# One weight's first step, two rests and one multiply moved on VectorE and GpSimd in the first MLP of a mixer and MLP kernel

## The chip, the cores and the metric

The kernel runs on one core of one Trainium2 chip. A core has a matrix engine (TensorE, called PE in the profile, with PEld for its weight loads), a vector engine (VectorE, DVE), an activation engine (ScalarE, ACT), GpSimd (POOL) and a queue engine that issues the transfers (SyncE, SP). Each works through its own instructions in order and waits for others by semaphores. The metric is the device time of one execution in microseconds (us), the median of several runs.

## The reference, cut to what matters

Three stages run behind each other on 4 batches: a gated linear attention with 8 heads of 48 columns over 768 steps, a mixer with a channel MLP of 1536 columns, and a gated spatial MLP.

```python
def _attn_ref(q, k, v, alpha):
    for t in range(S):
        state = alpha[:, :, t, :, None] * state + einsum('bhd,bhe->bhde', k[:, :, t], v[:, :, t])
        y[:, :, t] = einsum('bhd,bhde->bhe', q[:, :, t], state)

def _moe_ref(x, U, V, w_ch1, w_ch2):
    xt = x.transpose(0, 2, 1)
    h = xt @ U @ V
    u = x + h.transpose(0, 2, 1)
    ch = np.maximum(u @ w_ch1, 0.0) @ w_ch2
    return u + ch

def _moe2_ref(x, w_in, w_spatial, b_spatial, w_out):
    h = np.maximum(x @ w_in, 0.0)
    u, v = h[..., :512], h[..., 512:]
    v_n = (v - mean(v)) / np.sqrt(var(v) + 1e-06)
    v_s = einsum('ts,bsd->btd', w_spatial, v_n) + b_spatial[None, :, None]
    return (u * v_s) @ w_out
```

## The kernel before, in words

**Attention.** The 8 heads of a batch are 4 pairs of heads, so there are 16 pairs n, and batch 1 has the pairs 4 to 7 (in this text its first to fourth pair). `prepare(n)` makes running products of alpha: a scan backwards (`bw`, L914) with a reciprocal behind it (L917), and a scan forwards (`fw`, L927). `scale` (L903) multiplies k by `bw` and q by `fw`, on VectorE or on GpSimd: the variable `cut` says how much of it VectorE takes. In batch 1 VectorE takes k of the first three pairs and q of the third; GpSimd takes k of the fourth and q of the others. A pair then goes through PE in steps: k is turned (L958), what each chunk adds is made (L1002), VectorE scans it over the chunks (`state`, six scans, L1013), ScalarE lays the states out (L1023, L1024), PE makes scores (L974), VectorE masks them (L1091 for the third pair on, L984 before), and PE makes the outputs (L1103), which ScalarE takes (L1059). In the same steps the mixer of the pair before runs: two turns (L1213, taken by L1220), a product with U (L1229) into the bank that is called ALONE, and `keep`, which reads that bank on ScalarE (L1236) and VectorE (L1237). The turn of the next pair's k (L958) writes into ALONE as well, so it waits for L1237; L1229 waits for the six scans L1013, which read their decay out of ALONE.

**First MLP.** While batch 0's channel MLP runs on PE (up L380, ReLU L387 on ScalarE, the rest of h in `hl` L368 on VectorE, down L287 to L289, sum L440), the twelve weights come in as words of 64 bits and are made into two parts each, by hand-written steps. `begin` of a weight makes its 32-bit form on VectorE in three instructions (L237, L240, L247). `finish` is called twice for a weight: the first time ScalarE makes the high part (L785), the second time VectorE makes the rest (L252). L252 has both of its inputs in SBUF, and so has a multiply in L903.

**What sets the order.** The MLP calls `pull()` after every few matmuls, some 110 times and more in batch 0. At a pull (a hand-out) the table `FIRST_STEPS` says which weight steps are issued (`f` a finish, `b` a begin, `s` a step of the first batch's rest), and behind them, from pull 71 on, the steps of batch 1's attention are dealt out. Nothing reorders afterwards: each engine works in this order. The last `begin`, the twelfth weight's, is at pull 101, and the last three `finish` calls are at 107, 110 and 110. The eleventh weight's parts are called w_1459 and the twelfth's w_1619 in the lists below.

## Time and profile before

| what | before |
|---|---|
| median of 3 runs | 673.28 us (672.82 to 673.53) |
| the profiled execution | 674.17 us |
| its span, first to last instruction | 672.5 us |
| PE busy in the span | 658.3 us, 98% |
| VectorE, ScalarE, GpSimd busy | 425.3, 305.9 and 146.2 us |
| mean granted clock of TensorE | 0.997 of full speed |

The profile is of one execution, 0.89 us above the median of the runs. Times of rows count from the start of its span; 1.67 us of its time lie around the span. PE is busy nearly all the time, so what counts is where it is idle and who ends that. A row of the timeline has start, length, engine, line, operation, output and input tiles, shape and count; in brackets the idle time of the engine before it and what ended it. On VectorE an instruction's start is often recorded some 0.08 us before the one ahead of it ends.

### The profile page before, as it was taken

Reading aid. Unit: us, or ns where it says so; the run is one execution under the profiler, and the core shown is the slowest. Engines: PE = TensorE matmul, PEld = TensorE weight load, DVE = VectorE, ACT = ScalarE, POOL = GpSimd, SP = SyncE. Lnnn points to the kernel's source line nnn. Section 1 sums busy time; section 2 is a strip of 40 time slices with the busy share of each in tenths; the row PEclk is TensorE's granted clock in tenths of the full one; section 3 lists DMA queues with packets and bytes.
Section 4 is the critical chain, followed back from the end, with each engine's and each line's share of the span. In section 5 each row is a group of like instructions: output and inputs, shape, how many; then the busy total and the mean of one; then the engine's idle time right before and its main releaser. Section 6 shows DMA issues by size and latency. Waiting matters only on the chain.

```text
span 672.5 us, 13771 instructions
## 1 busy us (share of the span) xinstructions
PE 658.3 (98%) x5644; PEld 626.1 (93%) x5644; DVE 425.3 (63%) x813; ACT 305.9 (45%) x599; POOL 146.2 (22%) x138
## 2 busy tenths in 40 slices
PE   8999999899999999999999999999999999999995
PEld 7889999799999999999999999899999989999995
DVE  7989999867566336465327787495384356537441
ACT  3985467566455335555323444343344243334321
POOL 4530111232211231220110000306402520640141
PEclk9999999999999999999999999999999999999998
DMA  9699015562556502503023365401120202110011
GB/s 347 250 352 238 21 36 115 106 124 90 117 102 136 102 0 70 115 3 85 17 71 96 116 177 141 130 0 36 37 70 1 71 2 70 37 36 35 1 37 40
DMA packets 24039, 61.02 MB, mean 91 GB/s; under 512 B 3232, under 2 KB 13344, under 8 KB 22688
## 3 DMA queue, kind: packets, MB, share of 16 engines
q1 hardware_dynamic: 23968, 60.06, 32.6%
q8 instruction: 46, 0.75, 0.5%
q14 instruction: 25, 0.20, 0.1%
HBM read 47.47 MB, written 9.44 MB: 85 GB/s over the span
## 4 chain that ended last, share of the span: by engine, by line
PE 84%; DVE 8%; DMA 5%; issue 1%; ACT 1%; DVEq 0%; ACTq 0%; SPq 0%
PE banks L380 19%; PE banks L287 18%; PE banks L288 18%; PE banks L289 18%; DMA akq<-in_akq 5%; PE banks L1103 2%; DVE bw L914 1%; DVE fw L927 1%; PE banks L958 1%; PE banks L1002 1%; PE banks L974 1%; PE banks L1213 1%; PE banks L1175 1%; PE banks L1122 1%; DVE hl L368 1%
## 5 line engine op out<-in xcount | busy, mean ns | idle before, releaser
L380 PE MATMUL banks<-partuh,w 128*128 128x384 f32 x564 | 130.7, 339 | 1.4 <-DVE hl L368 1.3
L380 PEld LDWEIGHTS banks<-partuh,w 128*128 128x128 f32 x564 | 99.3, 188 | 3.5 <-DVE hl L368 2.2
L287 PE MATMUL banks<-h,w 128*128 128x384 f32 x288 | 98.1, 341 | 0.2
L289 PE MATMUL banks<-hl,w 128*128 128x384 f32 x288 | 96.4, 335 | 0.0
L288 PE MATMUL banks<-h,w 128*128 128x384 f32 x288 | 96.4, 335 | 0.0
L368 DVE SCALAR_TENSOR_TENSOR hl<-banks,h 128x384 fp32r<-128x384 f32 x96 | 52.7, 550 | 52.7 <-ACT h L387 52.1
L387 ACT ACTIVATE h<-banks 128x384 fp32r<-128x384 f32 x94 | 45.6, 486 | 76.4 <-PE banks L380 76.2
L252 POOL TENSOR_TENSOR partul<-ub,partuh 128x384 fp32r<-128x384 f32 x43 | 43.1, 1028 | 137.2 <-ACT partuh L457 84.7
L252 POOL TENSOR_TENSOR room<-room 128x384 fp32r<-128x384 f32 x32 | 32.5, 1017 | 163.2 <-ACT room L600 162.9
L380 PE MATMUL banks<-partul,w 128*128 128x384 f32 x282 | 66.1, 342 | 0.0
L287 PEld LDWEIGHTS banks<-h,w 128*128 128x128 f32 x288 | 54.1, 188 | 1.6 <-issue 0.8
L288 PEld LDWEIGHTS banks<-h,w 128*128 128x128 f32 x288 | 54.1, 188 | 0.0
L289 PEld LDWEIGHTS banks<-hl,w 128*128 128x128 f32 x288 | 54.1, 188 | 0.0
L903 POOL TENSOR_TENSOR akq<-akq,fw 128x768 f32<-128x768 f32 x13 | 22.5, 1730 | 135.1 <-DVE fw L927 86.6
L380 PEld LDWEIGHTS banks<-partul,w 128*128 128x128 f32 x282 | 49.2, 188 | 0.8
L600 ACT ACTIVATE room<-room 128x384 fp32r<-128x384 f32 x32 | 16.8, 526 | 66.8 <-DVE room L598 66.8
L252 DVE TENSOR_TENSOR vl<-vt,vh 128x512 fp32r<-128x512 f32 (+1 forms) x48 | 26.6, 617 | 20.7 <-ACT vh L505 20.7
L903 POOL TENSOR_TENSOR akq<-akq,bw 128x768 f32<-128x768 f32 x11 | 18.6, 1689 | 65.1 <-DVE bw L914 47.5
L289 PE MATMUL banks<-partul,winh 128*128 128x384 f32 x96 | 32.5, 338 | 0.0
L288 PE MATMUL banks<-partuh,winl 128*128 128x384 f32 x96 | 32.5, 338 | 0.0
L287 PE MATMUL banks<-partuh,winh 128*128 128x384 f32 x96 | 32.4, 338 | 0.0
L288 PE MATMUL banks<-wouth,room 128*128 128x384 f32 x96 | 32.3, 336 | 0.0
(256 smaller groups left out, 1498.3 us busy)
## 6 DMA issues: line engine op xcount, KB each, us to landing
akq<-in_akq SPq DMA_DIRECT2D x24, 434.4 KB, 7.6
bits<-in_w SPq DMA_DIRECT2D x12, 768.0 KB, 11.8
x2d<-ub SPq DMA_DIRECT2D x8, 576.0 KB, 3.4
ub<-x2d SPq DMA_DIRECT2D x8, 576.0 KB, 4.3
out_y<-room SPq DMA_DIRECT2D x24, 192.0 KB, 1.9
v<-in_v SPq DMA_DIRECT2D x15, 288.0 KB, 8.3
words<-in_wsT SPq DMA_DIRECT2D x7, 576.0 KB, 4.0
words<-in_w_in SPq DMA_DIRECT2D x8, 384.0 KB, 3.2
```

The lines of the kernel that those rows point to most:

```text
L252: engine.tensor_tensor(out=out, in0=x, in1=hi.bitcast(F32), op=ALU.subtract)
L287: nc.tensor.matmul(out=ps, lhsT=wh, rhs=xh, start=first, stop=False, skip_group_check=more)
L288: nc.tensor.matmul(out=ps, lhsT=wl, rhs=xh, start=False, stop=False, skip_group_check=more)
L289: nc.tensor.matmul(out=ps, lhsT=wh, rhs=xl, start=False, stop=last, skip_group_check=more)
L368: nc.vector.scalar_tensor_tensor(out=hl, in0=ps[:, 0:TB], scalar=0.0, in1=h.bitcast(F32), op0=ALU.max, op1=ALU.subtract)
L380: nc.tensor.matmul(out=ps[:, 0:TB], lhsT=wx[:, k * 128 : (k + 1) * 128], rhs=ux[:, k, :], start=i == 0, stop=i == len(parts) - 1)
L387: nc.scalar.activation(out=h, in_=ps[:, 0:TB], func=AF.Relu)
L600: nc.scalar.activation(out=hi, in_=x, func=AF.Copy)
L903: engine.tensor_tensor(out=chunks(x)[:, c], in0=chunks(x)[:, c], in1=chunks(by)[:, c, 1:CW], op=ALU.mult)
L914: nc.vector.tensor_tensor_scan(out=bw[:, ::-1], data0=a[:, 1 : AW + 1][:, ::-1], data1=ends[:, ::-1], initial=0.0, op0=ALU.mult, op1=ALU.max)
L927: nc.vector.tensor_tensor_scan(out=fw, data0=a[:, 0:AW], data1=starts, initial=0.0, op0=ALU.mult, op1=ALU.max)
L1103: nc.tensor.matmul(out=self.py[HW * h : HW * h + D, x, j * CH : (j + 1) * CH], lhsT=vw[:, h, c, :], rhs=self.sms[h][:, t], start=True, sto ...
```

## The change

The table hands out the last `begin` at pull 107 instead of 101, the rest of the eleventh weight at 110 instead of 107, and the rest of the twelfth at 113 instead of 110. The condition in `scale` gives VectorE the multiply of q by `fw` for the fourth pair too.

```diff
 FIRST_STEPS = {
     5: "f", 6: "b", 13: "fbf", 22: "fbf", 31: "fbf", 34: "ss", 40: "fbf", 49: "fbf", 51: "ss", 58: "f", 59: "f",
-    60: "b", 70: "ff", 80: "b", 89: "ff", 92: "b", 101: "fb", 107: "f", 110: "ff",
+    60: "b", 70: "ff", 80: "b", 89: "ff", 92: "b", 101: "f", 107: "b", 110: "ff", 113: "f",
 }
...
-            cut = NCH if n == 0 or by is bw and NP <= n < 2 * NP - 1 or by is fw and n == NP + 2 else 0
+            cut = NCH if n == 0 or by is bw and NP <= n < 2 * NP - 1 or by is fw and NP + 2 <= n < 2 * NP else 0
```

The first place is VectorE between the sums of the MLP (L440) and the correction L1237 of the first mixer product. Before:

```order
L440 TENSOR_TENSOR ub<-banks,ub 128x384 x3
L237 TENSOR_SCALAR narrow<-bits 128x768
L240 SCALAR_TENSOR_TENSOR narrow<-bits,narrow 128x768
L247 ISA narrow<-bits,narrow 128x1536
L1013 SCALAR_TENSOR_TENSOR after<-add,banks 128x96 x6
L1091 TENSOR_TENSOR akq_89<-banks,causal 64x6x64 x2
L1091 TENSOR_TENSOR sq<-banks,causal 64x6x64 x2
L368 SCALAR_TENSOR_TENSOR hl<-banks,h 128x384
L927 SCALAR_TENSOR_TENSOR fw<-akq_87,starts 128x780
L252 TENSOR_TENSOR w_1459<-narrow,w_1459 128x768
L1237 TENSOR_TENSOR stk<-banks,stk 32x128
```

The same place on VectorE in the changed kernel (akq_87 holds the fourth pair's k and q, akq_89 the third's):

```order
L440 TENSOR_TENSOR ub<-banks,ub 128x384 x3
L1013 SCALAR_TENSOR_TENSOR after<-add,banks 128x96 x6
L1091 TENSOR_TENSOR akq_89<-banks,causal 64x6x64 x2
L1091 TENSOR_TENSOR sq<-banks,causal 64x6x64 x2
L368 SCALAR_TENSOR_TENSOR hl<-banks,h 128x384
L927 SCALAR_TENSOR_TENSOR fw<-akq_87,starts 128x780
L903 TENSOR_TENSOR akq_87<-akq_87,fw 128x768
L237 TENSOR_SCALAR narrow<-bits 128x768
L240 SCALAR_TENSOR_TENSOR narrow<-bits,narrow 128x768
L247 ISA narrow<-bits,narrow 128x1536
L1237 TENSOR_TENSOR stk<-banks,stk 32x128
```

The three rows of the begin went from ahead of the six scans to behind the scan L927, the multiply L903 came in ahead of them, and L252 left the place ahead of L1237.

The second place is VectorE behind L1237, up to the fourth pair's scans and masks. Before:

```order
L1237 TENSOR_TENSOR stk<-banks,stk 32x128
L252 TENSOR_TENSOR w_1619<-narrow,w_1619 128x768
L368 SCALAR_TENSOR_TENSOR hl<-banks,h 128x384
L440 TENSOR_TENSOR ub<-banks,ub 128x384 x3
L914 SCALAR_TENSOR_TENSOR bw<-akq_88,ends 128x780
L917 RECIPROCAL starts<-bw 128x12
L1013 SCALAR_TENSOR_TENSOR after<-add,banks 128x96 x6
L1091 TENSOR_TENSOR akq_87<-banks,causal 64x6x64 x2
```

The same place in the changed kernel (akq_88 holds k and q of pair 8, the first of batch 2):

```order
L1237 TENSOR_TENSOR stk<-banks,stk 32x128
L252 TENSOR_TENSOR w_1459<-narrow,w_1459 128x768
L368 SCALAR_TENSOR_TENSOR hl<-banks,h 128x384
L440 TENSOR_TENSOR ub<-banks,ub 128x384 x3
L914 SCALAR_TENSOR_TENSOR bw<-akq_88,ends 128x780
L917 RECIPROCAL starts<-bw 128x12
L252 TENSOR_TENSOR w_1619<-narrow,w_1619 128x768
L1013 SCALAR_TENSOR_TENSOR after<-add,banks 128x96 x6
L1091 TENSOR_TENSOR akq_87<-banks,causal 64x6x64 x2
```

The rest of the eleventh weight now stands behind L1237, and that of the twelfth between pair 8's scan L914 and the fourth pair's scans L1013. On GpSimd the multiply of akq_87 by `fw` is gone and nothing else moves; the orders of PE, ScalarE and SyncE are what they were.

## Rows read from the trace of the kernel before

**Rows 1.** Stretch table: stretch, its length, busy of PE, PEld, DVE, ACT, POOL, clock, DMA.

```profile
143.00:665.00 522.00, 521.73 (x3934) 503.23 (x3933) 294.38 (x610) 212.42 (x422) 113.75 (x104) 1.00 0.25 67
```

**Rows 2.** Timeline of PE, 117 to 138 us, third and fourth pair.

```profile
117.60 0.93 PE L974 MATMUL banks<-akq 64*64 64x64 f32 x48
...
120.23 1.55 PE L1229 MATMUL banks<-yb,u 128*96 128x128 f32 x12 [0.98 <-DVE after L1013]
...
122.75 0.23 PE L1103 MATMUL banks<-akq,state 128*48 128x64 f32 x1 [0.37 <-DVE sq L1091]
...
127.51 0.84 PE L958 MATMUL banks<-ident,akq 128*128 128x128 f32 x6 [0.50 <-DVE stk L1237]
...
129.40 0.34 PE L289 MATMUL banks<-hl,w 128*128 128x384 f32 x1
...
137.34 0.23 PE L1103 MATMUL banks<-akq,state 128*48 128x64 f32 x1
```

**Rows 3.** Timeline of DVE, 116 to 134 us.

```profile
116.15 0.55 DVE L237 TENSOR_SCALAR narrow<-bits 128x768 uint32<-128x768 uint32 x1
...
118.61 1.57 DVE L1013 TENSOR_TENSOR_SCAN after<-add,banks 128x96 f32<-128x96 f32 x6
120.21 1.22 DVE L1091 TENSOR_TENSOR akq<-banks,causal 64x384 f32<-64x384 f32 x2
...
123.95 0.56 DVE L368 SCALAR_TENSOR_TENSOR hl<-banks,h 128x384 fp32r<-128x384 f32 x1 [1.35 <-ACT h L387]
124.42 1.77 DVE L927 TENSOR_TENSOR_SCAN fw<-akq,starts 128x780 f32<-128x780 f32 x1
126.11 0.93 DVE L252 TENSOR_TENSOR w<-narrow,w 128x768 fp32r<-128x768 f32 x1
127.08 0.28 DVE L1237 TENSOR_TENSOR stk<-banks,stk 32x128 fp32r<-32x128 f32 x1
127.77 1.64 DVE L252 TENSOR_TENSOR w<-narrow,w 128x768 fp32r<-128x768 f32 x1 [0.41 <-ACT w L785]
...
131.31 1.77 DVE L914 TENSOR_TENSOR_SCAN bw<-akq,ends 128x780 f32<-128x780 f32 x1
133.11 0.23 DVE L917 RECIPROCAL starts<-bw 128x12 f32<-128x12 f32 x1
133.26 1.51 DVE L1013 TENSOR_TENSOR_SCAN after<-add,banks 128x96 f32<-128x96 f32 x6
```

**Rows 4.** Timeline of ACT, 115 to 127 us.

```profile
115.44 0.70 ACT L1010 ACTIVATE add<-banks 128x576 f32<-128x576 f32 x1
120.21 1.14 ACT L1023 ACTIVATE state<-after 64x528 f32<-64x528 f32 x1 [4.07 <-DVE after L1013]
...
123.45 0.47 ACT L387 ACTIVATE h<-banks 128x384 fp32r<-128x384 f32 x1
...
126.22 0.27 ACT L1236 ACTIVATE stk<-banks 96x128 fp32r<-96x128 f32 x1
```

**Rows 5.** Timeline of DVE, the third pair's `fw` and q.

```profile
109.25 1.77 DVE L927 TENSOR_TENSOR_SCAN fw<-akq,starts 128x780 f32<-128x780 f32 x1
111.05 0.96 DVE L903 TENSOR_TENSOR akq<-akq,fw 128x768 f32<-128x768 f32 x1
111.93 0.55 DVE L368 SCALAR_TENSOR_TENSOR hl<-banks,h 128x384 fp32r<-128x384 f32 x1
```

**Rows 6.** Timeline of POOL: the fourth pair's q, and pair 8's k.

```profile
126.36 2.23 POOL L903 TENSOR_TENSOR akq<-akq,fw 128x768 f32<-128x768 f32 x1 [10.37 <-DVE fw L927]
133.21 1.68 POOL L903 TENSOR_TENSOR akq<-akq,bw 128x768 f32<-128x768 f32 x1 [4.62 <-DVE bw L914]
```

**Rows 7.** Timeline of POOL in the last stage.

```profile
467.52 1.98 POOL L654 TENSOR_TENSOR late<-late,bb 128x384 f32<-128x384 f32 x2
```

**Rows 8.** Timeline of DVE at the same time.

```profile
468.56 1.35 DVE L593 TENSOR_TENSOR room<-late 128x384 f32<-128x384 f32 x1 [1.73 <-POOL late L654]
```

**Rows 9.** What line L593 runs: count, ns least/median/most, first and last start, form.

```profile
L593 DVE TENSOR_TENSOR room<-late x8: 548/951/1357, 468.6 to 652.0; 128x384 f32<-128x384 f32 x8
```

## The prediction

> **What bounds the kernel now.** I read the stretch table first, then the timelines of PE, VectorE, ScalarE and GpSimd around 116 to 138 us, where the change lies. From 143 us to 665 us PE is busy for 521.73 of 522.00 us [rows 1]: whatever PE loses or wins before 143 us moves the end by the same amount, and nothing later takes it back. So the question is what the change does to PE's waits in the third and fourth pair of batch 1. There are three [rows 2]: 0.98 us ahead of the mixer product L1229 (for the six scans L1013), 0.37 us in the outputs L1103 (for the masks L1091), and 0.50 us ahead of the turn L958 (for L1237). The reader should see that all three releasers are VectorE rows, and that VectorE runs from 116.15 us to 127.36 us with one hole of 1.35 us, in which it waits for h [rows 3]. Here VectorE's queue sets the pace, not PE.
>
> **The begin, taken away ahead of the scans.** Its three instructions lie between 116.15 and 118.61 us, 2.46 us [rows 3]. Without them the scans can start when `add` is there: ScalarE's L1010 ends at 115.44 + 0.70 = 116.14 us [rows 4], so they start at about 116.17 us, 2.44 us earlier, and end at 117.74 us. L1229 then waits for nothing: PE is ready at 120.23 - 0.98 = 119.25 us. The masks need the scores, which end at 117.60 + 0.93 = 118.53 us [rows 2] and don't move; two pairs of masks take 123.95 - 1.35 - 120.21 = 2.39 us [rows 3], so they end at 120.96 us instead of 122.60, and the 0.37 us goes too. PE is then at the turn L958 some 0.98 + 0.37 = 1.35 us earlier, at 127.51 - 0.50 - 1.35 = 125.66 us or before. If that were all, the gain would be up to 0.98 + 0.37 + 0.50 = 1.85 us.
>
> **What it meets at L1237.** The turn L958 waits for L1237, and the begin now stands ahead of L1237, with one more multiply. Follow VectorE's queue. ScalarE starts its chain on the end of the scans (L1023 at 120.21 us, h at 123.45 us [rows 4]); all of it comes 2.44 us earlier, so `hl` L368 starts at 123.95 - 2.44 = 121.51 us, later than the masks' end and so still set by h. The scan L927 starts at 124.42 - 2.44 = 121.98 us. Multiplying q on VectorE is priced from the third pair [rows 5]: the multiply starts 111.05 - 109.25 = 1.80 us behind its scan and the next instruction 0.88 us behind that, so 123.78 and 124.66 us. The begin takes 2.46 us from there: L1237 starts at 127.12 us. Before it started at 127.08 us [rows 3]. In one sum: 2.44 us earlier into the chain, the rest L252 out of the way (127.08 - 126.11 = 0.97 us), and 0.94 us of multiply (the 0.88 us, and the 0.06 us more that an instruction waits which needs the scan's result) and 2.46 us of begin come in: +0.05 us or so. L1236 on ScalarE ended at 126.49 us [rows 4], some 0.6 us before L1237, and comes earlier now, so it doesn't decide. PE's turn starts at 127.55 us against 127.51 us, and the two waits that vanished come back as one of about 1.9 us in front of L958. Queued behind it on PE are the rest of the weight steps' matmuls and the fourth pair. **This part is worth nothing, 0.0 within 0.1 us.** The 0.1 is what single starts on VectorE differ by in rows of the same kind.
>
> **q of the fourth pair off GpSimd.** GpSimd's multiply took 2.23 us, 126.36 to 128.59 us [rows 6], and goes. Its readers are the scores, which PE runs behind the turn L958, and the copy of q into `sq` on SyncE's queue, which L1103 reads later still; the copy, and the loads queued behind it there, may start some 4 us earlier (124.7 instead of 128.6 us), but with the turn where it was an earlier q helps no one. But it had cost VectorE something: the rest L252 at 127.77 us took 1.64 us against 0.93 us for the same form at 126.11 us [rows 3], and it ended at 129.41 us, 0.82 us behind the multiply's end. So one of them stood still while the other ran. That 0.71 us goes, but PE doesn't wait there.
>
> The Trainium skill says of elementwise work (GPSIMD Engine Reference, Engine selection) that VectorE should have it, GpSimd being about 2 times slower on two inputs. The rows agree, 0.96 against 1.68 to 2.23 us; by that rule the move would gain 0.7 us or more, by the row of PE's wait it gains nothing, since VectorE is the engine that is short here.
>
> **The two rests.** w_1459's L252 now follows L1237, from about 127.3 to 128.3 us. Its reader, the eleventh weight's third group of matmuls, is ordered behind the second mixer turn and L1002, so it has time. `hl` and the three sums L440 follow; the last sum needs L289, which PE ends at 129.40 + 0.34 = 129.74 us [rows 2], 129.78 us now. From there pair 8's scan L914 can start at some 130.28 us (one sum's spacing is 0.46 us), a good 1 us before its 131.31 us [rows 3], and ends at 130.28 + 1.77 = 132.05 us.
>
> Now comes the place that decides. On the end of L914 GpSimd starts to multiply pair 8's k: 133.21 us, 0.13 us behind 131.31 + 1.77 = 133.08 us [rows 6], so at 132.18 us. VectorE's second instruction behind L914 starts 0.18 us behind it (L1013 at 133.26 us, 0.15 us behind L917's start [rows 3]), so at 132.23 us. Before, that was L1013, which reads one input from PSUM and ran along undisturbed. Now it is w_1619's L252, the very instruction that stood still beside GpSimd in the row above. Two bounds:
>
> - GpSimd comes first: L252 ends 0.82 us behind GpSimd's end, at 132.18 + 1.68 + 0.82 = 134.68 us, and the fourth pair's scans start 0.08 us before that, at 134.60 us instead of 133.26: 1.34 us later. Behind them on VectorE stand the four masks, and who waits for those is L1103. Before, scans and masks end at 133.26 + 1.51 + 0.03 + 2.39 = 137.19 us, and the L1103 that needs the last mask starts at 137.34 us [rows 2], 0.15 us behind it, just as at 122.60 and 122.75 us in the third pair: there is no room, and PE goes on 1.34 us later.
> - VectorE comes first: the scans start at 132.23 + 0.86 = 133.09 us, 0.17 us earlier, GpSimd waits, and nobody needs pair 8's k until the next batch. PE is then as before, 0.0 to -0.1 us.
>
> I take the first. GpSimd's start is 0.05 us ahead by the rows, and where the two came close in the last stage, GpSimd's second multiply (from about 468.49 to 469.50 us [rows 7]) was some 0.07 us ahead of VectorE's L593 at 468.56 us, and it was VectorE that stood: 1.35 us [rows 8] where the same form takes 0.55 us [rows 9]. But 0.05 us is the smallest lead of all, and both starts are worked out.
>
> The Trainium skill has the rule behind these rows (SBUF — State Buffer, Who interferes with whom): a VectorE instruction with two SBUF inputs and a GpSimd one that reads SBUF need the same port, and "Issue order, not op shape, decides who blocks." The trace agrees that one blocks whole (1.64 against 0.93 us); by the rule the sum is +1.34 us where GpSimd issues first. Another page (Perfetto Trace Analysis, DVE / Act Engine Instruction) says that VectorE's recorded start lies behind the start of its reading; no run here shows it, and by it the lead may be none and the sum 0.0 us.
>
> **The sum.** 0.0 us at L958 and +1.34 us at the fourth pair's scans. The profiled execution took 674.17 us, so 675.5 us; against the median, 673.28 + 1.34 = 674.6 us. That is slower by 0.199%, just at the 0.2% that a measurement of this kernel can tell from no change.
>
> **The rivals.**
>
> - *VectorE takes the port first.* Place: w_1619's L252 beside pair 8's k at 132.2 us. Price: 1.34 us less than the forecast, so 673.2 us, not slower. It decides within some 0.05 us: if L252 reads before GpSimd does. For it: the lead is tiny, and worked out from starts that may not mean the same on two engines. Against: rows 7 to 9.
> - *The chain to L1237 is shorter than worked out*, and part of the three waits is won: up to 1.85 us, 671.4 us; with L252 stalled as well, 672.8 us. For it: three edits at once, and PE is ready 1.9 us ahead. Against: every term of the queue has its row, and to win 1 us it would have to run a microsecond faster than it did.
> - *More is lost than the stall*: the start of the fourth pair's h and the first products of the mixer come late beyond the 1.34 us because ScalarE, too, gets out of step. Some 0.5 us more, 675.1 us. Nothing in the rows asks for it.
>
> That the instructions don't move as said is excluded by the lists of their order.
>
> **How the numbers follow.** Forecast 0.52, VectorE first 0.36, a shorter chain 0.06, more lost 0.06. The range goes from 672.8 us (VectorE first, less the 0.1 us of the chain and some 0.3 us of what runs differ by) to 675.2 us (the forecast and half a microsecond); it leaves out most of the third case and part of the last. Slower by over 0.2%: half of the forecast, 0.26, and most of the last, 0.05, so 0.31 in all. Within 0.2%: the other half, VectorE first, some of the third: 0.64. Faster: 0.05. The forecast's own range is 674.2 to 675.1 us.
>
> **What the profile after would show.** Right: PE's waits ahead of L1229 and L1103 of the third pair gone, one of some 1.9 us ahead of L958 at 127.5 us; L1237 at about 127.1 us behind L247; an L252 of about 2.4 us behind L917, and the fourth pair's scans at 134.6 us, with a new wait of PE in L1229 or L1103. Wrong: L252 there at 0.9 us and GpSimd's multiply at 2.4 us or so (then VectorE was first), or L1237 well before 127 us (then the queue was mis-sized, and the time falls).

## The result, and the profile after

The changed kernel takes 676.52 us (median of 8 runs, 675.77 to 680.10) where the kernel before, run beside it, takes 673.46 us (8 runs, 672.82 to 674.01): a ratio of 1.0058, 95% interval 1.0047 to 1.0070. It is slower by 3.1 us; the forecast was 674.6 us, in a range up to 675.2. Beside the later experiments it was 676.80 against 674.00 us, 1.0047 (1.0035 to 1.0059). The kernel before has few runs above 675 us in any comparison; the changed kernel has none below 675.5 in 15, and they spread far wider.

| what | before | after |
|---|---|---|
| the profiled execution | 674.17 us | 675.77 us |
| its span | 672.5 us | 674.1 us |
| PE busy in the span | 658.3 us | 658.5 us |
| mean granted clock of TensorE | 0.997 | 0.995 |

In the trace after, everything from 10 us to 110 us is some 0.3 us later than in the trace before, since the first input load came later; times below are as recorded, so 0.3 us of each difference is that.

PE first, from the third pair's end on (start, length, engine, line, operation, tiles, count, idle time ahead and who ended it):

```profile
119.44 1.47 PE L1229 MATMUL banks<-yb,u 128*96 128x128 f32 x12
...
121.46 0.23 PE L1103 MATMUL banks<-akq,state 128*48 128x64 f32 x1 [0.30 <-DVE sq L1091]
...
128.07 1.51 PE L958 MATMUL banks<-ident,akq 128*128 128x128 f32 x6 [2.36 <-DVE stk L1237]
129.37 0.85 PE L1213 MATMUL banks<-ident,ub 128*128 128x128 f32 x3
129.87 0.67 PE L287 MATMUL banks<-h,w 128*128 128x384 f32 x1
130.34 0.52 PE L288 MATMUL banks<-h,w 128*128 128x384 f32 x1
...
131.26 0.33 PE L288 MATMUL banks<-h,w 128*128 128x384 f32 x1
...
135.20 1.21 PE L974 MATMUL banks<-akq 64*64 64x64 f32 x48
```

Against [rows 2] the wait of 0.98 us ahead of L1229 is gone, that in L1103 is 0.30 instead of 0.37 us, and that ahead of L958 is 2.36 us instead of 0.50, for the same releaser, L1237. So far this is the exchange that was worked out. What comes behind was not: the turn L958 takes 1.51 us instead of 0.84, and L288 0.52 us where it takes 0.33 from 131.26 us on. The stretch table says why (stretch, its length, busy of PE, PEld, DVE, ACT, POOL, granted clock, DMA share, GB/s):

```profile
112.00:125.70 13.70, 13.40 (x207) 12.12 (x206) 12.00 (x23) 10.43 (x21) 1.69 (x1) 1.00 0.62 125
125.70:128.00 2.30, 0.00 (x1) 0.00 (x0) 2.20 (x4) 0.37 (x2) 0.00 (x0) 0.95 0.63 133
128.00:130.00 2.00, 1.93 (x10) 1.96 (x10) 1.93 (x3) 1.36 (x3) 0.00 (x0) 0.50 1.14 279
130.00:132.00 2.00, 2.00 (x11) 2.00 (x10) 0.75 (x2) 0.60 (x2) 0.00 (x0) 0.70 0.86 158
132.00:143.00 11.00, 11.00 (x191) 10.09 (x190) 9.06 (x16) 7.20 (x13) 2.61 (x2) 1.00 0.27 48
```

The granted clock was 1.00 (2.4 GHz) until PE stood idle from 125.70 us on, fell to 0.50 (1.2 GHz) just ahead of 128 us, and was back at 1.00 by 131.2 us. Between the two, PE does all it has to do, at half speed.

The last line of the first table is less plain: 48 matmuls of L974 took 1.21 us, where before the same row is 0.93 us, at 133.13 us. Inside it the 44th starts at 135.90 us and the 45th at 136.08, 0.18 us apart, where before they are 0.04 us apart. That small hole is the edge of the second cause, below.

VectorE, GpSimd, and the queue of SyncE in the changed kernel:

```profile
116.52 1.58 DVE L1013 TENSOR_TENSOR_SCAN after<-add,banks 128x96 f32<-128x96 f32 x6
...
126.65 0.96 DVE L247 CUSTOM_DVE_ANT_0 narrow<-bits,narrow 128x1536 uint16<-128x1536 uint16 x1
127.64 0.28 DVE L1237 TENSOR_TENSOR stk<-banks,stk 32x128 fp32r<-32x128 f32 x1
...
131.22 1.15 DVE L440 TENSOR_TENSOR ub<-banks,ub 128x384 f32<-128x384 f32 x2 [1.25 <-PE banks L289]
...
134.09 0.23 DVE L917 RECIPROCAL starts<-bw 128x12 f32<-128x12 f32 x1
134.24 0.90 DVE L252 TENSOR_TENSOR w<-narrow,w 128x768 fp32r<-128x768 f32 x1
135.05 1.57 DVE L1013 TENSOR_TENSOR_SCAN after<-add,banks 128x96 f32<-128x96 f32 x6
```

```profile
134.19 2.47 POOL L903 TENSOR_TENSOR akq<-akq,bw 128x768 f32<-128x768 f32 x1 [17.93 <-DVE bw L914]
```

```profile
125.22 0.50 SPq L1080 DMA_DIRECT2D sq<-akq  x1
125.82 1.18 SPq L1083 DMA_DIRECT2D state<-in_v  x2
127.04 1.05 SPq L855 DMA_DIRECT2D akq<-in_akq  x2
128.13 0.42 SPq L856 DMA_DIRECT2D v<-in_v  x1
```

L1237 starts at 127.64 us, 0.2 us later than the 127.12 + 0.3 worked out; half of that is that it follows L247 by 0.99 us, where the instruction behind L247 followed it by 0.88 us before. Beside pair 8's multiply it was VectorE that got through: L252 took 0.90 us, and GpSimd 2.47 instead of the 1.68 us of [rows 6]. And SyncE issues the copy of q and the loads behind it from 125.22 us on. In the kernel before the same four rows are:

```profile
128.62 0.50 SPq L1080 DMA_DIRECT2D sq<-akq  x1
129.22 1.18 SPq L1083 DMA_DIRECT2D state<-in_v  x2
130.44 1.05 SPq L855 DMA_DIRECT2D akq<-in_akq  x2
131.53 0.42 SPq L856 DMA_DIRECT2D v<-in_v  x1
```

These 3.4 us turned out to matter, too.

### The profile page after: what moved, and what is told of

It is laid out like the page before. It is cut to its first block, busy times and chain, and to the rows that moved or that the text cites. A ratio compares the mean times of both kernels' runs of the same rounds, so it can differ in the third digit from the quotient of the medians.

```text
span 674.1 us, 13769 instructions
## 1 busy us (share of the span) xinstructions
PE 658.5 (98%) x5644; PEld 626.8 (93%) x5644; DVE 425.8 (63%) x814; ACT 306.4 (45%) x599; POOL 144.8 (21%) x137
## 4 chain that ended last, share of the span: by engine, by line
PE 82%; DVE 12%; ACT 3%; issue 2%; DMA 0%; DVEq 0%; ACTq 0%
PE banks L380 19%; PE banks L287 18%; PE banks L288 18%; PE banks L289 18%; PE banks L1103 2%; DVE fw L927 2%; DVE bw L914 2%; PE banks L1002 1%; PE banks L974 1%; DVE narrow L240 1%; PE banks L958 1%; DVE narrow L247 1%; PE banks L1213 1%; DVE hl L368 1%; PE banks L1229 1%
## 5 line engine op out<-in xcount | busy, mean ns | idle before, releaser
L380 PE MATMUL banks<-partuh,w 128*128 128x384 f32 x564 | 130.7, 339 | 1.5 <-DVE hl L368 1.3
L380 PEld LDWEIGHTS banks<-partuh,w 128*128 128x128 f32 x564 | 99.3, 188 | 3.6 <-DVE hl L368 2.3
L289 PE MATMUL banks<-hl,w 128*128 128x384 f32 x288 | 96.6, 335 | 0.0
L288 PE MATMUL banks<-h,w 128*128 128x384 f32 x288 | 96.6, 335 | 0.0
L368 DVE SCALAR_TENSOR_TENSOR hl<-banks,h 128x384 fp32r<-128x384 f32 x96 | 52.7, 550 | 52.4 <-ACT h L387 51.7
L252 POOL TENSOR_TENSOR partul<-ub,partuh 128x384 fp32r<-128x384 f32 x43 | 43.2, 1029 | 138.0 <-ACT partuh L457 84.9
L252 POOL TENSOR_TENSOR room<-room 128x384 fp32r<-128x384 f32 x32 | 32.6, 1018 | 163.1 <-ACT room L600 162.8
L380 PE MATMUL banks<-partul,w 128*128 128x384 f32 x282 | 66.1, 342 | 0.0
L288 PEld LDWEIGHTS banks<-h,w 128*128 128x128 f32 x288 | 54.3, 189 | 0.0
L289 PEld LDWEIGHTS banks<-hl,w 128*128 128x128 f32 x288 | 54.2, 188 | 0.0
L380 PEld LDWEIGHTS banks<-partul,w 128*128 128x128 f32 x282 | 49.2, 188 | 0.8
L903 POOL TENSOR_TENSOR akq<-akq,fw 128x768 f32<-128x768 f32 x12 | 20.3, 1690 | 124.4 <-DVE fw L927 71.5
L252 DVE TENSOR_TENSOR vl<-vt,vh 128x512 fp32r<-128x512 f32 (+1 forms) x48 | 26.6, 617 | 20.7 <-ACT vh L505 20.7
L903 POOL TENSOR_TENSOR akq<-akq,bw 128x768 f32<-128x768 f32 x11 | 19.4, 1762 | 78.7 <-DVE bw L914 64.8
L288 PE MATMUL banks<-partuh,winl 128*128 128x384 f32 x96 | 32.4, 338 | 0.0
L289 PE MATMUL banks<-partul,winh 128*128 128x384 f32 x96 | 32.4, 338 | 0.0
L288 PE MATMUL banks<-wouth,room 128*128 128x384 f32 x96 | 32.3, 336 | 0.0
```

The costliest lines, as they stand in the source:

```text
L252: engine.tensor_tensor(out=out, in0=x, in1=hi.bitcast(F32), op=ALU.subtract)
L288: nc.tensor.matmul(out=ps, lhsT=wl, rhs=xh, start=False, stop=False, skip_group_check=more)
L289: nc.tensor.matmul(out=ps, lhsT=wh, rhs=xl, start=False, stop=last, skip_group_check=more)
L368: nc.vector.scalar_tensor_tensor(out=hl, in0=ps[:, 0:TB], scalar=0.0, in1=h.bitcast(F32), op0=ALU.max, op1=ALU.subtract)
L380: nc.tensor.matmul(out=ps[:, 0:TB], lhsT=wx[:, k * 128 : (k + 1) * 128], rhs=ux[:, k, :], start=i == 0, stop=i == len(parts) - 1)
L903: engine.tensor_tensor(out=chunks(x)[:, c], in0=chunks(x)[:, c], in1=chunks(by)[:, c, 1:CW], op=ALU.mult)
```

## The experiments

Two theories stood at the start. **Clock**: the long wait lets TensorE's clock fall, and that costs more than the wait. **Waits alone**: the clock is a symptom, and VectorE's queue and GpSimd's port decide. A third, **code**, came out of the first traces. Times of before are those beside each run. PE's lateness in a trace is told against the trace of the kernel before.

### One part of the change at a time

The steps moved, q of the fourth pair left on GpSimd:

```diff
-            cut = NCH if n == 0 or ... or by is fw and NP + 2 <= n < 2 * NP else 0
+            cut = NCH if n == 0 or ... or by is fw and n == NP + 2 else 0
```

> The table of steps as changed, but q of the fourth pair multiplied on GpSimd again. VectorE's queue to L1237 is one multiply (0.94 us) shorter than in the changed kernel, so PE should be idle some 1.3 to 1.5 us ahead of L958 instead of 2.36. Theory 'clock' (the long idle time takes TensorE's clock to its lower level, which costs more than the idle time itself): if 1.4 us is short enough, the granted clock stays at 1.00 from 127 to 132 us and L958 takes 0.84 us; then PE gains 0.9 us of wait and some 1.7 us of slow clock on the changed kernel, at most, and the time is 673 to 674 us. If 1.4 us is too long too, the clock falls and the time is some 0.9 us under the changed kernel, 675.6 us. Rival 'waits alone' (the clock costs nothing): 0.9 us under the changed kernel, 675.6 us. The stretch of the fourth pair's scans still has L252 beside GpSimd's multiply of pair 8.

Measured: 676.03 us (674.87 to 677.26) against 674.12, ratio 1.0033 (1.0021 to 1.0044). The wait didn't shrink; it grew to 2.72 us:

```profile
124.85 2.32 DVE L240 SCALAR_TENSOR_TENSOR narrow<-bits,narrow 128x768 uint32<-128x768 uint32 x1
...
128.63 0.85 PE L958 MATMUL banks<-ident,akq 128*128 128x128 f32 x6 [2.72 <-DVE stk L1237]
```

The begin's L240 reads two tiles in SBUF, met GpSimd's multiply of q (124.54 us, 1.82 us), and took 2.32 us instead of 0.96. So moving q to VectorE takes 0.36 us off this wait, which I had not asked of it: it takes GpSimd away from the begin. In the time that doesn't show: with q left on GpSimd the median lies 1.9 us above that of before, with q moved 2.8 to 3.1 us. In this execution, the fastest of its six, the clock stayed at 1.00 behind a wait of 2.72 us. The length of the wait alone doesn't decide whether it falls.

Only q moved, the steps as before:

```diff
-    60: "b", 70: "ff", 80: "b", 89: "ff", 92: "b", 101: "f", 107: "b", 110: "ff", 113: "f",
+    60: "b", 70: "ff", 80: "b", 89: "ff", 92: "b", 101: "fb", 107: "f", 110: "ff",
```

> The table of steps as before, and only q of the fourth pair moved to VectorE. 0.94 us come in ahead of L1237 and PE's wait ahead of L958 goes from 0.50 to some 1.4 us; the 0.71 us that L252 of w_1619 lost beside GpSimd come back behind it. Theory 'clock': if 1.4 us lets the clock fall, L958 takes about 1.5 us and the time is 1 to 2.5 us above the kernel before (674.5 to 676); if not, the clock stays 1.00. Rival 'waits alone': at most +0.9 us, and since VectorE has 0.71 us back by the fourth pair's masks, +0.2 us there, 673.5 to 674.4 us.

Measured: 675.19 us (674.09 to 675.61) against 674.12, 1.0013 (1.0004 to 1.0022). PE's wait is 1.52 us, 1.02 more than before, the clock stays at 1.00, and the loss is 1.07 us. The half of the expectation that had VectorE give it back by the masks was wrong: there VectorE now waits 0.30 us for PE's scores.

### PE kept busy while it waits

Nine matmuls of 128 columns into an unread place, ahead of the turn:

```diff
+                if n == 2 * NP - 1:
+                    busy(9, ps.banks[:, PAIR[0], :])
                 pair.flip()
```

> The changed kernel, and nine matmuls of 128 columns (2 us) into an unread place of a bank put on PE ahead of the turn L958, so that PE works while it would wait for L1237. Nothing else moves. Theory 'clock': the granted clock stays at 1.00 from 128 to 131 us, L958 takes 0.84 us instead of 1.51, L287 behind it 0.33 us a matmul instead of 0.5 to 0.67, PE is 1.7 us ahead from 132 us on, and the time is 1.2 to 1.9 us under the changed kernel (674 to 675.3 us). Rival 'waits alone': the dummies only fill the wait, 0.0 to +0.2 us against the changed kernel. A second rival, that VectorE is late at the fourth pair whatever PE's clock is, has PE gain the 1.7 us at 132 us and give it back as a wait in L1103 by 138 us.

Measured: 674.22 us (673.30 to 674.67) against 674.12, 0.9998 (0.9989 to 1.0006). All that the change had lost is back, for nine matmuls whose result nobody reads:

```profile
125.83 2.17 PE L939 MATMUL banks<-ident 128*128 128x128 f32 x18
128.34 0.85 PE L958 MATMUL banks<-ident,akq 128*128 128x128 f32 x6 [0.33 <-DVE stk L1237]
```

"Waits alone" falls. It looked as if the clock were the whole story; it is not, since half speed from 127.8 to 131.2 us can cost 1.7 us, and 2.8 to 3.1 are lost. Nor does this run separate the clock from the third theory: the load of code that matters below came early in it, too (124.70 us).

### The weight's rest and GpSimd's port

The twelfth weight's rest behind the fourth pair's masks, out of GpSimd's way:

```diff
-    ... 107: "b", 110: "ff", 113: "f",
+    ... 107: "b", 110: "ff", 118: "f",
```

> The changed kernel, with the rest of w_1619 handed out at 118 instead of 113, so that its L252 stands behind the fourth pair's masks and not between pair 8's scan L914 and the fourth pair's scans. L958, its wait and the clock are as in the changed kernel. Theory 'port': in some executions of the changed kernel L252 stands beside GpSimd's multiply and the fourth pair comes 1.34 us later; here it can't, so the runs lie closer together than the 675.8 to 680.1 us of the changed kernel, and its median falls by 0.5 to 1.3 us, to about 675.5. Rival: the spread has another source (the clock), and stays; then 676 to 676.6 us.

Measured: 676.95 us (675.36 to 678.56) against 674.12, 1.0043 (1.0028 to 1.0058). Median and spread stay, so the port is not where they come from. But its trace shows a wait that no engine ends ("issue"), 0.76 us, between the 44th and the 45th matmul of the fourth pair's scores, at 136.63 us.

The opposite, VectorE held back a little by a second L917, so that GpSimd reads first:

```diff
-            nc.vector.reciprocal(out=starts[:, 0 : AW : AW // n_c], in_=pe)
+            for _ in range(2 if n == 2 * NP else 1):
+                nc.vector.reciprocal(out=starts[:, 0 : AW : AW // n_c], in_=pe)
```

> The changed kernel, with the reciprocal L917 of pair 8 issued twice, which puts VectorE's w_1619 L252 some 0.15 to 0.2 us later against GpSimd's multiply of pair 8's k, so that GpSimd reads first. PE's wait ahead of L958 and the clock are as in the changed kernel. Theory 'the port decides by who reads first': L252 takes some 2.4 us instead of 0.90, GpSimd 1.7 us instead of 2.47, the fourth pair's scans start 1.5 us later, and the time is 1.0 to 1.5 us above the changed kernel's 676.5. Rival 'VectorE always goes first there': L252 stays at 0.90 us and the time at +0.2 us.

Measured: 677.81 us (676.79 to 679.24) against 674.26, 1.0054 (1.0040 to 1.0068); with the lines below 917 one further down, its profiled run of 679.24 us has:

```profile
133.53 2.18 DVE L252 TENSOR_TENSOR w<-narrow,w 128x768 fp32r<-128x768 f32 x1
...
135.64 1.56 DVE L1014 TENSOR_TENSOR_SCAN after<-add,banks 128x96 f32<-128x96 f32 x6
```

```profile
133.22 1.68 POOL L903 TENSOR_TENSOR akq<-akq,bw 128x768 f32<-128x768 f32 x1 [16.96 <-DVE bw L914]
```

```profile
128.56 0.85 PE L959 MATMUL banks<-ident,akq 128*128 128x128 f32 x6 [2.35 <-DVE stk L1238]
...
134.21 0.92 PE L975 MATMUL banks<-akq 64*64 64x64 f32 x44
137.30 0.33 PE L975 MATMUL banks<-akq 64*64 64x64 f32 x4 [2.17 <-issue]
137.56 0.59 PE L287 MATMUL banks<-h,w 128*128 128x384 f32 x1
137.94 0.52 PE L288 MATMUL banks<-h,w 128*128 128x384 f32 x1
```

The port does what the prediction priced: with 0.31 us of lead GpSimd keeps its 1.68 us, L252 takes 2.18, and the scans start 2.11 us behind its start instead of 0.81, which is 1.30 us (1.34 were worked out). Yet it is not what cost the time. The clock stayed at 1.00 behind L958; PE came early to the fourth pair's scores, stood 2.17 us at the same 45th matmul, and there the clock fell (0.52 to 0.59 us a matmul behind it). VectorE's masks waited 0.46 us for these scores, not the other way round.

### The 45th matmul: PE's code

What ends these waits is in the list of transfers. PE's instructions come in loads of 16 KB in a queue of their own, q8, 46 loads in the run. The page of after has (queue, kind, packets, MB, share):

```profile
q8 instruction: 46, 0.75, 0.5%
```

The Trainium skill (Runtime: NRT & Kernel Launch, Instruction fetch mechanics) says that an engine's code is streamed in blocks of 16 KiB, 256 instructions, by a DMA queue of the engine's sequencer while the page before is executed, mostly hidden. The counts agree: 5644 matmuls and as many weight loads make some 44 such blocks. That q8 is PE's follows from this count, from the table, and from a run further down, in which the place moves with the code. The table sets the one load of q8 that lies in this place beside the start of L958 and of the 45th matmul:

| kernel | copy of q (L1080) issued | L958 starts | load of q8 | 45th of L974 starts | behind the load |
|---|---|---|---|---|---|
| before | 128.62 | 127.51 | 124.44 to 125.59 | 133.83 | |
| after | 125.22 | 128.07 | 132.90 to 134.61 | 136.08 | 1.47 |
| after, measured again | 125.17 | 128.02 | 133.29 to 134.89 | 136.20 | 1.31 |
| after, third trace | 125.45 | 128.29 | 132.72 to 134.24 | 135.65 | 1.41 |
| rest behind the masks | 125.06 | 127.90 | 133.84 to 135.41 | 136.63 | 1.22 |
| GpSimd first | 125.72 | 128.56 | 134.34 to 135.96 | 137.30 | 1.34 |
| loads late (below) | 128.44 | 127.90 | 129.09 to 130.51 | 134.22 | |

In each of these five with a late load the 45th matmul starts 1.22 to 1.47 us behind its end, and in no trace whose load ended more than 1.5 us ahead of the 45th is there a hole at that place. In the five the load starts 4.4 to 5.9 us behind L958, among the input loads that SyncE has issued since some 125 us; where these go out later it starts 1.2 us behind L958. All traces fit one order. Where SyncE issues the two loads of akq (L855, 434 KB each) behind the start of L958, q8's load starts ahead of L958 or 1.2 to 1.8 us behind it. Where it issues them ahead of L958, q8's load starts 3.1 to 5.9 us behind, but for the kept-busy kernel, which had it ahead of both. So it takes the early loads and PE's long wait together: with the wait but late loads ("loads late") there is no hole, and with early loads but no wait (the begin right behind L1237, below) there is none either. Why the kernel before has it ahead of L958 at all, with the same instructions on PE, the traces don't tell.

The changed kernel again:

> The changed kernel once more, for a second trace of it and beside the next two on one chip. What spread its runs over 675.8 to 680.1 us is open. Theory 'code': besides the slow clock behind PE's wait at L958, PE runs out of code at the 45th matmul of the fourth pair's scores L974, because its 16 KB load lands late among the input loads that now go out 3.4 us earlier; the wait there differs between executions, and where it is long the clock may fall once more. A profiled run near the median (676.5) should then show a wait of 0.5 to 1.5 us in L974 that no other engine's row ends, right behind the end of a load of the instruction queue. Rival 'clock alone': nothing in L974, and two falls of the clock or a longer one in the slower runs.

Measured: 676.80 us (675.50 to 677.92) against 674.00. Its trace (676.45 us) has the slow clock behind L958 (0.52 from 128 to 130 us), a hole of 0.2 us at the 45th matmul instead of the 0.5 to 1.5 expected, and 0.60 us at 420 us, where L380 waits for VectorE's L368, which is late behind a step that waited for a load of the next stage's weights (L708).

Nine matmuls of one column, to move PE's code as the nine wide ones did, without keeping PE busy:

```diff
+                if n == 2 * NP - 1:
+                    for _ in range(9):
+                        nc.tensor.matmul(out=ps.banks[:, PAIR[0], 511:512], lhsT=g["ident"], rhs=g["ident"][:, 0:1], start=True, stop=True)
                 pair.flip()
```

> The changed kernel with nine matmuls of one column ahead of the turn L958, at the same place as the nine wide ones of the run that kept PE busy. They move PE's code by as much, but leave PE idle for about 2 us. Theory 'clock': the wait still ends in a slow clock, in some or all executions, and the time stays 1 us or more above the kernel before (675 to 676.5). Theory 'code': the load that came late in the changed kernel now goes out ahead of the wait, near 124.7 us as in the kept-busy kernel, there is no wait in L974, and the runs lie within 1.5 us of each other; whatever is left above the kernel before is the wait and the clock. If it is as fast as the kernel before, the clock costs nothing and the kept-busy result was all code.

Measured: 675.35 us (673.56 to 676.65) against 674.00, 1.0016 (1.0006 to 1.0025). In its trace (676.65 us) the load is as late as in the changed kernel, 133.44 us, and the clock falls (0.62 and 0.52 from 128 to 132 us). So moving the code doesn't bring the load forward, and what did so in the kept-busy kernel (124.70 us there) was something else. But the run shows that the hole is code. The nine matmuls count as 18 in the trace, and the hole, small again, is now 18 matmuls earlier, between the 26th and the 27th:

```profile
135.58 0.68 PE L974 MATMUL banks<-akq 64*64 64x64 f32 x26
136.45 0.57 PE L974 MATMUL banks<-akq 64*64 64x64 f32 x22 [0.19 <-issue]
```

The load of q8 ended at 134.99 us, 1.46 us ahead. What the 27th and the 45th matmul share is their place in PE's instructions, not their data.

SyncE's queue held back until L1237, so that the copy of q and the input loads go out when they did before:

```diff
+                    if n + 1 == 2 * NP - 1:
+                        late = cp.tile([R, 1], F32, name="late", tag="late1")
+                        nc.sync.dma_start(out=late, in_=stk[R : 2 * R, mix.m * 128 : mix.m * 128 + 1].bitcast(F32))
                     placed[n + 1] = WholePair(n + 1, None, None, tags)
```

> The changed kernel, with one transfer of 32 numbers that needs L1237 put into SyncE's queue ahead of the copy of q, so that this copy and the input loads behind it go out at about 128.5 us, as in the kernel before (128.62), and not at 125.2. PE's wait at L958 (2.36 us) and VectorE's order stay. Theory 'code': PE's load, asked for when L958 gets through, is ahead of most of the input loads, ends by 132 us, PE has no wait in L974, the spread of the runs goes, and the median falls by 0.5 to 1.0 us, to some 675.5, where the wait and the slow clock remain. Rival 'clock alone': no change in median or spread (676.5).

Measured: 674.24 us (673.31 to 676.15) against 674.00, 1.0006 (0.9997 to 1.0015). One transfer of 32 numbers takes 2.6 us off the changed kernel (676.80), more than expected. The same kernel, traced again:

> The kernel with the late loads again, one look. Its runs lay between 673.3 and 676.2 us, and its first trace, at 673.55, had PE idle for 2.36 us and the clock at 1.00 behind it. Theory: the clock falls behind that wait in some executions only, and these are the slow ones: where the trace shows 0.50 behind L958, the time is 674.9 us or more; where it shows 1.00, 674.4 or less; in both, no wait in L974. Rival: slow ones differ in another place.

> The same kernel, one more look, with the same expectation: clock 0.50 behind L958 and 674.9 us or more, or clock 1.00 and 674.4 us or less.

> The same kernel, one more look, with the same expectation: clock 0.50 behind L958 and 674.9 us or more, or clock 1.00 and 674.4 us or less.

Measured: 674.39, 673.72 and 674.23 us (before, beside them: 674.11). The clock fell in the first and the third and stayed in the second, as it had stayed in the trace at 673.55 us. First the trace at 673.55 us, then the one at 674.39:

```profile
127.90 0.84 PE L958 MATMUL banks<-ident,akq 128*128 128x128 f32 x6 [2.36 <-DVE stk L1237]
```

```profile
128.22 0.99 PE L958 MATMUL banks<-ident,akq 128*128 128x128 f32 x6 [2.34 <-DVE stk L1237]
129.01 0.85 PE L1213 MATMUL banks<-ident,ub 128*128 128x128 f32 x3
129.51 0.67 PE L287 MATMUL banks<-h,w 128*128 128x384 f32 x1
```

The same wait, with the clock at 1.00 behind one and 0.50 behind the other. But the two executions in which it fell lie 0.5 and 0.7 us under the 674.9 expected, and near the others. The reason is a side effect: in all four traces of this kernel PE's matmuls from 142 us to the end take 0.65 to 1.1 us less than before. The small extra tile shifts what lies behind it in SBUF; that this is the cause was not shown. So of the 2.6 us some 0.9 don't belong to the place in question. Nor does a fall of the clock show in full in the times of these four: behind PE's last matmul the two in which it fell are 0.6 to 0.8 us shorter than the other two, for a reason that stays open.

And the changed kernel, traced again:

> The changed kernel, a third trace. Theory: the load of PE's code ends at 134.5 us or later, 6 us or more behind the start of L958, and the 45th matmul of L974 starts 1.2 to 1.5 us behind that end; if the clock falls behind L958 (0.50), PE comes there late and waits 0.2 to 0.8 us; if the clock stays at 1.00, PE comes early and waits about 2 us. The time is 675.5 us or more in both cases.

Measured: 675.94 us against 674.11. The clock stayed at 1.00, and PE stood for its code:

```profile
128.00:130.00 2.00, 1.71 (x13) 1.74 (x14) 1.94 (x4) 1.87 (x4) 0.00 (x0) 1.00 0.99 230
```

```profile
128.29 0.85 PE L958 MATMUL banks<-ident,akq 128*128 128x128 f32 x6 [2.36 <-DVE stk L1237]
...
133.92 0.91 PE L974 MATMUL banks<-akq 64*64 64x64 f32 x44
135.65 0.33 PE L974 MATMUL banks<-akq 64*64 64x64 f32 x4 [0.82 <-issue]
```

So the traces divide the loss. How late PE is at the first of the six L1213 that start at 141.42 us before, less how late it already was at the third pair's scores (117.60 us before), ahead of everything that the change moved on PE. That start is -0.02 to +0.57 us in these traces and differs between executions of one kernel:

| input loads | clock stayed behind L958 | clock fell behind L958 |
|---|---|---|
| early (the changed kernel) | +1.23 | +1.85, +2.01 |
| late | +0.07, +0.08 | +1.66, +1.62 |

So the exchange of waits that the change makes is worth 0.1 us; the kept-busy kernel, with neither the slow clock nor the hole, is at +0.07, too. The clock alone costs 1.5 to 1.6 us, the late code alone 1.2, and both together only 1.8 to 1.9: with a slow clock PE comes to the 45th matmul when its code is nearly there. The three traced executions of the changed kernel took 1.8 to 2.5 us more than the medians of before beside them, and this place and the start make that up to within 0.2 us. The medians of the changed kernel lie 2.8 to 3.1 us above; what its slower executions have beyond this was not traced.

### The wait by itself

In the kernel before, the scan L927 of the fourth pair issued twice, 1.78 us more of VectorE ahead of L1237 and nothing else:

```diff
-            nc.vector.tensor_tensor_scan(out=fw, data0=a[:, 0:AW], data1=starts, initial=0.0, op0=ALU.mult, op1=ALU.max)
+            for _ in range(2 if n == 2 * NP - 1 else 1):
+                nc.vector.tensor_tensor_scan(out=fw, data0=a[:, 0:AW], data1=starts, initial=0.0, op0=ALU.mult, op1=ALU.max)
```

> The kernel before, with the scan L927 of the fourth pair issued twice: 1.78 us more of VectorE ahead of L1237 and nothing else. PE's wait ahead of L958 goes from 0.50 to some 2.28 us, as long as in the changed kernel, but with q of the fourth pair on GpSimd and the steps where they were. Theory 'clock': the granted clock falls behind the wait in some or all executions, L958 takes 1.5 us in these, and the time is 1.8 us (clock kept) to 3.6 us (clock fallen) above the kernel before, with runs spread over both. Rival 'waits alone': +1.8 us and runs as close as before.

Measured: 676.46 us (675.71 to 676.97) against 674.26, 1.0033 (1.0021 to 1.0045): +2.2 us, between the two expectations. In its trace the clock fell, and PE went from +1.98 us at L958 to +3.56 at the first L974 behind it:

```profile
129.49 1.32 PE L959 MATMUL banks<-ident,akq 128*128 128x128 f32 x6 [2.32 <-DVE stk L1238]
...
131.10 0.67 PE L287 MATMUL banks<-h,w 128*128 128x384 f32 x1
131.56 0.52 PE L288 MATMUL banks<-h,w 128*128 128x384 f32 x1
```

So a wait of 2.3 us can bring the slow clock with q on GpSimd, too, and it costs 1.6 us in the execution where it comes.

### Can the exchange be kept and the wait avoided?

The begin right behind L1237 instead of right ahead:

```diff
-    ... 101: "f", 107: "b", 110: "ff", 113: "f",
+    ... 101: "f", 108: "b", 110: "ff", 113: "f",
```

> The changed kernel with the last begin handed out at 108 instead of 107, which puts its three instructions right behind L1237 instead of right ahead. L1237 should start near 125.1 us and PE's wait ahead of L958 go from 2.36 us to under 0.3, with the clock at 1.00 throughout. VectorE still has all its work ahead of the fourth pair's scans: L1013 of that pair at about 134 us, against 135.05 in the changed kernel and 133.26 before. Theory 'clock': 2 us or more below the changed kernel (673.5 to 675 us), with the close runs of the kernel before. Rival 'VectorE's queue alone': the wait comes back at the fourth pair, and only 1.0 us is won (675.5).

Measured: 674.42 us (674.09 to 674.92) against 674.26, 1.0000 (0.9990 to 1.0010). One hand-out further and the kernel is level with the one before, with the closest runs of all. PE reaches L958 at 125.94 us without a wait, the clock stays, its code lands at 127.64 to 128.60 us. Of the 1.57 us that it is ahead there, 0.43 are left at the second mixer turn L1213 and 0.07 at the fourth pair's scores: ScalarE's L785 waits for the begin, ahead of kn (L961). Then PE waits 0.37 us for the fourth pair's masks, where it didn't before, and at 141.42 us it is, the start taken off, 0.1 us late.

```profile
129.68 0.55 PE L1213 MATMUL banks<-ident,ub 128*128 128x128 f32 x3 [1.00 <-ACT kn L961]
```

Both rests moved into holes of VectorE as well:

```diff
-    ... 101: "f", 107: "b", 110: "ff", 113: "f",
+    ... 101: "f", 105: "f", 108: "b", 110: "f", 118: "f",
```

> A version made from the readings so far. The begin goes behind L1237 (108), w_1459's rest into VectorE's hole behind the third pair's masks (105), w_1619's rest behind the fourth pair's masks and L368 (118), q of the fourth pair stays on VectorE. Expected: L1229 without a wait, L1103 at 0.3 us, L958 under 0.3 us, clock 1.00, the fourth pair's scans near 132.1 us instead of 133.26 before, PE some 1.0 to 1.3 us ahead of the kernel before from 138 us on, and the time 0.8 to 1.3 us below it (about 0.15%). If the loads of the next batch or ScalarE hold it, 0.0.

Measured: 674.00 us (673.09 to 674.56) against 674.26, 0.9997 (0.9988 to 1.0006). The fourth pair's scans start at 132.16 us as expected, but the 1.00 us ahead of L1213 is there again. With the first finish of the twelfth weight at 115 instead of 110, so that L785 comes behind kn:

```diff
-    ... 108: "b", 110: "f", 118: "f",
+    ... 108: "b", 115: "f", 118: "f",
```

> The version with three moves, with the first finish of the twelfth weight (L785 on ScalarE) handed out at 115 instead of 110, so that ScalarE takes kn (L961) before it waits for the begin. In the version with three moves PE waited 1.00 us for L961 ahead of L1213; this should go, and come back in part as a wait for the fourth pair's masks, since VectorE was only some 0.3 us from deciding there. Expected 0.3 to 0.6 us below the version with three moves, 0.5 to 0.8 us below the kernel before (673.5 where before is 674.2).

Measured: 674.07 us (672.90 to 674.50) against 674.00, 1.0001 (0.9992 to 1.0010). That wait went, and two others came:

```profile
136.23 0.23 PE L1103 MATMUL banks<-akq,state 128*48 128x64 f32 x1 [0.37 <-DVE sq L1091]
...
138.93 0.79 PE L380 MATMUL banks<-partuh,w 128*128 128x384 f32 x3 [0.54 <-DVE w L252]
```

PE is 1.63 us ahead of the kernel before at the fourth pair's scores and 0.28 ahead at the L1213 behind them: the masks, and the weight's own rest, which is now too late, take it back. A wait of 0.60 us at 417.65 us, the one named at 420 us above, takes the rest. No version made here beats the kernel before.

## Why the prediction was wrong, point by point

- **What bounds the kernel: right up to PE's last matmul.** In the trace after PE is 2.20 us late at 143.6 us and 2.27 at its last matmul. Behind that 0.6 us come back, since the end of the run is shorter than in the one trace of the kernel before.
- **The begin taken away: right.** L1013 at 116.52 us (116.17 and the 0.3 of the start), no wait ahead of L1229. The 0.37 us in L1103 didn't go but shrank to 0.30: PE comes there earlier, too, so the same two engines meet as before.
- **What it meets at L1237: right in kind.** 127.64 us against 127.12 + 0.3, and one wait of 2.36 us where about 1.9 was said.
- **"This part is worth nothing, 0.0 within 0.1 us": the step that failed, in two ways.** First, it priced PE's waits by their length, three short ones against one long one. The clock was 1.00 behind waits of up to 1.10 us before, and falls behind 2.36 us in some executions, which costs 1.5 to 1.6 us. TensorE's clock is not in the prediction at all. Second, it has the loads behind the copy of q start some 4 us earlier, which they did (3.4 us), and says that this helps no one. It harms: PE's code lands among them, and PE stands at the 45th matmul of L974 until 1.2 to 1.5 us behind the end of that load, which costs 1.2 us where the clock stays. A transfer that comes early was costed at nothing without asking what else goes through the same engines then. With the loads late and the clock up, two traces show what the prediction had worked out: 0.1 us.
- **q off GpSimd: not worth nothing.** Left there, it meets the begin's L240 (2.32 us instead of 0.96) and makes PE's wait 0.36 us longer; but with q on GpSimd the copy of q goes out later (126.39 us), PE's load of code ends at 133.32 us with no hole behind it, and the median lies 0.9 to 1.2 us less above that of before (the intervals touch).
- **The port at w_1619's L252: the rival held.** VectorE went first in all three traces of the changed kernel, with GpSimd's start recorded 0.04 to 0.05 us ahead. The forecast's +1.34 us was not in them. That the fourth pair's scans start at 135.05 us, near the 134.60 of the forecast, is luck: VectorE had stood 1.25 us for PE's L289, which ran at half speed. The price was right (1.30 us on VectorE with GpSimd ahead), but in the one trace that has it PE came 0.46 us later than the masks needed, so PE didn't pay it. The Trainium skill (SBUF — State Buffer, Who interferes with whom) makes issue order decide who blocks; the rows bear that out for a lead of 0.31 us, and show that at 0.05 us or less the recorded starts don't tell the order.
- **The sum.** 674.6 us was near to nothing that happened: its 1.34 us stood for a stall that didn't come, and what the traces show in its place, 1.2 to 2.0 us at 141 us, are two mechanisms that weren't among the rivals. The rival "more is lost" had 0.06 and only 0.5 us more.

**What stays open.** The three traces of the changed kernel are of 675.8 to 676.5 us; its executions of 677 to 680 us were not traced. The trace at 679.24 us with GpSimd first shows how one can come about (2.17 us for the code and a fall of the clock behind that), no more. A wait of 0.15 to 0.76 us near 420 us, behind a load of the next stage's weights, is in some traces of several kernels and not in that of the kernel before; it was not followed up. Nor is it known what decides in which execution the clock falls.

## What to carry to other kernels

Price a wait of the matrix engine by what stands behind it, too: waits of 0.98, 0.37 and 0.50 us merged into one of 2.36 us were no even exchange, since the clock can fall in it. Where an edit lets a bulk transfer start earlier, look at what else is loaded in that stretch, the engines' own code among it; a hole that ends for no engine ("issue") and lies right behind a load of the instruction queue, here 1.2 to 1.5 us behind its end, is that. And when a step is moved from the front of one critical instruction, put it behind the next one, not right in front: one hand-out further gave back what was lost.

## What the runs showed of the hardware

- The same wait of PE, 2.34 to 2.36 us at the same place, has the clock at 0.50 behind it in some executions and at 1.00 in others; once it stayed at 1.00 behind 2.72 us. Neither the code nor the length decides it alone.
- PE ran out of code for 0.2 to 2.2 us: 16 KB took 1.5 to 1.7 us to land among input loads, and started up to 5.9 us behind L958, where it starts 1.2 us behind when the input loads go out late.
- It isn't the only such place. In eight traces, ahead of all that the change moves on PE, one matmul near 108.6 us, 380 matmuls ahead of the 45th, comes 0.2 to 0.6 us late, 1.2 to 1.5 us behind the end of another load of q8. The Trainium skill's "mostly hidden" (Runtime: NRT & Kernel Launch, Instruction fetch mechanics) is so for most of the 46 loads, not for these. The row of the kernel with GpSimd first:

```profile
108.89 1.34 PE L1045 MATMUL banks<-akq,state 128*48 128x64 f32 x39 [0.38 <-issue]
```

- A second instruction with two inputs in SBUF, the begin's L240, stands beside GpSimd as L252 does: 2.32 us against 0.96.
